# Retention from block 8 on by chunks of 64 tokens, with the state stacked under the values, in a fused retention and maxout kernel

## The chip, the cores and the metric

One core of a Trainium2 chip runs the whole kernel. The metric is the time of one execution on the device, in microseconds (us). The engines are called as in the profile: PE is TensorE (PEld its weight loads), DVE VectorE, ACT ScalarE, POOL GpSimd and SP SyncE, which issues nearly all DMAs.

## What is computed

Eight sequences of 576 tokens with 8 heads of 64 go through retention: causal attention without softmax, in which a key that lies r tokens back is weighted by gamma to the power r. Its output, 4608 tokens by 512, is the input of a feed-forward layer that takes the largest of three products.

```python
def _attn_ref(q, k, v):                      # 8 x 8 x 576 x 64 each
    scores = scale * np.matmul(q, k.transpose(0, 1, 3, 2))
    gamma = 1.0 - 2.0 ** (-5.0 - np.arange(H))
    rel = pos[:, None] - pos[None, :]
    Dmat = np.where(rel >= 0, gamma[:, None, None] ** rel[None, :, :], 0.0)
    return np.matmul(scores * Dmat, v)

def _moe_ref(x, w1, w2, w3, w_out):          # x: 4608 x 512, w: 512 x 768, w_out: 768 x 512
    h = np.maximum(np.maximum(x @ w1, x @ w2), x @ w3)
    return h @ w_out
```

All data is fp32. The weights come as 64-bit floats and are converted in the kernel.

## The kernel before

**Blocks and tiles.** The 4608 tokens are 36 blocks g of C = 128; four blocks make one tile t of NT = 512 tokens, nine in all. Blocks do not line up with the sequences: a sequence is four and a half blocks. While the feed-forward work of tile t runs (`ffn`, L618), the retention of tile t + 1 is woven into it. `steps(t)` (L731) writes that order out by hand: twelve slots per tile, and the loop at the end (L771) runs the calls of a slot and then lets `ffn` go on to its next `yield`. From tile 1 on, 120 of PE's fp32 products, spread over six feature blocks `fb` of 20 each (`up`, L559), stand between slots 0 and 9; slots 10 and 11 lie in `downs` (L407). Nothing is reordered afterwards: each engine executes its instructions in the order in which this Python code issues them.

**Retention of one block before.** The decay is split into a factor of the key's position (`gk`), one of the query's position (`gq`), and a causal mask. `load` brings k, v (and, up to block 6, q) with tokens on the partitions; `load_blocks` (L187) brings q and k a second time in 32 by 32 blocks, so that DVE's block transpose gives `qT` and `kT` with the head's dimension on the partitions (`transposes`, L220; up to block 6 PE transposes instead). `decay_values` (L212) multiplies v by `gk` on POOL to give `vd`. `scores` (L236) makes eight products kT qT, 64 rows by 128 columns of weights with 128 columns moving, in two PSUM banks, and DVE multiplies each bank by the causal mask into `st`. `state` (L255) makes K^T vd, eight products with 64 columns moving, and `keep` (L266) adds it to the running state on DVE and multiplies the sum by gamma^128 (`gs`) on POOL. `values` (L284) makes the output of two blocks: `vd` times `st` (L299, eight products for each block), the next states' products (L263), and the state times `qT` (L312, eight for each block, over the queries whose sequence began in an earlier block); `output` multiplies the two banks by `gq` on DVE into `xT`, and after the last block of a tile adds the 13 sums of X that the fast matrix product of the feed-forward layer needs (L343).

**Who works when.** `soon` (L180) puts DVE steps of retention, and the loads, in a queue `urgent`; `chore` takes one out between products (L663 sets how often), and `scores` and `values` empty the queue first. `up` leaves its partial products in the banks of `ps_x` and `ps_y` (two each); ACT copies them to `part` tiles (20 in turn), and DVE joins these (L568). Retention has the four banks of `ps_r`.

Of the kernel before, what the change touches and what calls it, by code (L numbers as in the profile page):

```python
# [48 lines left out]
C = 128  # L49
NT = 4 * C  # L50
NH = NT // 2
BY_PE = 7
AHEAD = 3
FILL = 224
# [26 lines left out]
def kernel(  # L81
# [24 lines left out]
    assert B * S % C == 0 and S >= C and N % NT == 0 and NT % P == 0 and 2 * D == P and NP == NDC  # L106
# [3 lines left out]
    vpool = ctx.enter_context(tc.tile_pool(name="vpool", bufs=3))  # L110
    att = ctx.enter_context(tc.tile_pool(name="att", bufs=2))
    stp = ctx.enter_context(tc.tile_pool(name="stp", bufs=4))
# [15 lines left out]
    gk = const.tile([C, H], FP32, name="gk")  # L128
    one, top, inf, first = (const.tile([P, 1], FP32, name=n) for n in ("one", "top", "inf", "first"))
    const.tile([P, FILL // 4], FP32, name="fill")  # L130
    gq = const.tile([P, 2, NP // 2, C], FP32, name="gq")
    gs = const.tile([P, NP, D], FP32, name="gs")
# [18 lines left out]
    def start_of(g):  # L151
        r = -g * C % S
        return r if r < C else None

    masks = {0: causal, None: causal}
    for r in sorted({start_of(g) for g in range(NG)} - {0, None}):
        m = masks[r] = const.tile([C, C], FP32, name=f"causal{r}")
        nc.gpsimd.tensor_copy(m[:], causal[:])
        nc.gpsimd.memset(m[0:r, r:C], 0.0)


    raws, vds, qks, sts, states, kvs = {}, {}, {}, {}, {}, {}
# [10 lines left out]
    late, chores, urgent, spread = {}, deque(), deque(), []  # L173
# [13 lines left out]
    def load_blocks(g, *blocks):  # L187
        for n, src in (("q", q), ("kx", k)):

            if 0 in blocks:  # L190
                raws[n, g] = raw.tile([P, NP, C // 32, 32], FP32, tag=n, name=n + "raw", bufs=2)
            t = raws[n, g]
            for blk in blocks:
                b, pos = divmod(g * C + 32 * blk, S)
                for a in range(4):
                    nc.sync.dma_start(
                        t[32 * a:32 * a + 32, :, blk, :],
                        src[b, a // 2::2, pos:pos + 32, 32 * (a % 2):32 * (a % 2) + 32].rearrange("p j i -> j p i"))

    def load(g):  # L200
        if g >= BY_PE and ("q", g) not in raws:
            load_blocks(g, *range(C // 32))
        for n, src in (("k", k), ("q", q), ("v", v)) if g < BY_PE else (("k", k), ("v", v)):
            if n == "v" and g == CPT - 1:
                load_weights(1)
            bufs = 3 if n == "k" else 2
            pool, bufs = (raw0, 1) if g < BY_PE and g % (bufs + 1) == bufs else (raw, bufs)
            t = raws[n, g] = pool.tile([C, H, D], FP32, tag=n, name=n + "raw", bufs=bufs)
            for row, b, pos, m in spans(g):
                nc.sync.dma_start(t[row:row + m], src[b, :, pos:pos + m, :].rearrange("h p d -> p h d"))  # L210

    def decay_values(g):  # L212
        t = vds[g] = vpool.tile([C, H, D], FP32, tag="vd", name="vd")
        nc.gpsimd.tensor_tensor(t[:], raws.pop(("v", g))[:], gk[:].unsqueeze(2).to_broadcast([C, H, D]),  # L214
                                op=ALU.mult)
# [4 lines left out]
    def transposes(g):  # L220
        both = qks[g] = {}
        if g >= BY_PE:
            for n in ("k", "q"):
                t = both[n] = att.tile([P, NP, C], FP32, tag=n + "T", name=n + "T", bufs=2 if n == "k" else 3)
                soon(partial(nc.vector.transpose, t[:].rearrange("a p c -> a (p c)"),
                             raws.pop(("kx" if n == "k" else n, g))[:].rearrange("a p b i -> a (p b i)")))
            return
        for n, src in (("k", raws["k", g]), ("q", raws.pop(("q", g)))):
            pool, tag = (ps_r, "r") if g >= CPT else (ps_x, "x")
            pt = pool.tile([P, NP, C], FP32, tag=tag, name=n + "t")  # L230
            for p in range(NP):
                nc.tensor.transpose(pt[:, p, :], pair(src, p), ident[:C, :C])
            t = both[n] = att.tile([P, NP, C], FP32, tag=n + "T", name=n + "T", bufs=2 if n == "k" else 3)
            nc.scalar.copy(t[:], pt[:])

    def scores(g):  # L236
        chore(len(urgent))
        qT, kT = qks[g]["q"], qks[g]["k"]
        s = [ps_r.tile([C, NP, C], FP32, tag="r", name=f"s{j}") for j in range(2)]
        for p in range(NP):  # L240
            for j in range(2):
                r = slice(D * j, D * (j + 1))
                nc.tensor.matmul(s[j][:, p, :], lhsT=kT[r, p, :], rhs=qT[r, p, :], start=True, stop=True)  # L243
        st = sts[g] = att.tile([C, 2, NP, C], FP32, tag="st", name="st", bufs=2)
        for j in range(2):
            soon(partial(nc.vector.tensor_tensor, st[:, j], s[j][:],
                         masks[start_of(g)][:].unsqueeze(1).to_broadcast([C, NP, C]), op=ALU.mult))
# [4 lines left out]
    def half(j):  # L252
        return slice(D * j, D * (j + 1))
# [12 lines left out]
    def keep(g):  # L266
        def step(t, kv):
            if start_of(g) is not None:
                nc.vector.tensor_tensor(t[:], kv[:], gs[:], op=ALU.mult)
            else:  # L270
                nc.vector.tensor_tensor(t[:], kv[:], states[g][:], op=ALU.add)  # L271
                nc.gpsimd.tensor_tensor(t[:], t[:], gs[:], op=ALU.mult)  # L272

        if begins(g):
            t = states[g + 1] = stp.tile([P, NP, D], FP32, tag="state", name="state")
            soon(partial(step, t, kvs[g]))
# [7 lines left out]
    def values(chunks, new_states=(), later=False):  # L284
# [7 lines left out]
        t, i = divmod(chunks[0], CPT)  # L292
        pool, tag = (ps_r, "r") if chunks[0] >= CPT - 1 else (ps_y, "y")
        o = [pool.tile([P, len(chunks), NP // 2, C], FP32, tag=tag, name="o") for _ in range(2)]
        for m, g in enumerate(chunks):
            for n in range(NP):
                for c in range(2):
                    h = head(c, n)
                    nc.tensor.matmul(o[n % 2][half(c), m, n // 2, :], lhsT=vds[g][:, h, :],  # L299
                                     rhs=sts[g][:, h % 2, h // 2, :], start=m == 0 and n < 2,  # L300
                                     stop=before(g) == 0, skip_group_check=True)
# [20 lines left out]

    def output(chunks, o, t, i):
# [8 lines left out]
        i += len(chunks) - 1  # L332
# [285 lines left out]
    def ffn(t):  # L618
# [36 lines left out]
        for n, fb in enumerate(order):  # L655
            if fb not in plain:
                while fb // 2 not in summed_fp:
                    chore()
            steps_of_one = up_plain_all(t, h, fb) if fb in plain else up(t, h, fb)
            for step, cost in enumerate(steps_of_one):  # L660
                if fb in plain:
                    chore(4 if (fb, step) == (plain[-1], 1) else 8)
                elif step % 2 or step % 5 == 4:  # L663
                    chore(len(urgent) > 0)
                elif step % 4 == 2 and chores:
                    chores.popleft()()
                count += cost or 1
                if count * (NF // 2 * 3) >= (parts + 1) * total:
                    parts += 1
                    yield  # L670
            if n % 2:
                sums_of_hidden(h, fb // 2)
                if fb in plain:
                    weight_sums(fb // 2)
        chore(len(urgent))
        for n, _ in enumerate(downs(t, h)):
            chore(4)
            if n in (1, 3):
                yield
# [17 lines left out]
    decay_values(0)  # L697
# [7 lines left out]
    decay_values(1)  # L705
# [6 lines left out]
    decay_values(2)  # L712
# [4 lines left out]
    decay_values(3)  # L717
# [10 lines left out]
    decay_values(CPT)  # L728
    convert(2)

    def steps(t):  # L731
# [4 lines left out]
        def at(n, *what):  # L736
            for step, *args in what:
                if step is values:
                    if args[0][0] < NG:
                        todo[n].append(partial(values, args[0], [g for g in args[1] if g < NG]))  # L740
# [3 lines left out]
        if t == 1:  # L744
# [3 lines left out]
            at(2, (transposes, b), (decay_values, b), (load, c))  # L748
            at(3, (scores, b), (load_blocks, d, 0))
            at(4, (decay_values, c), (load_blocks, d, 1, 2))  # L750
            at(5, (values, [a, b], [b, c]), (load_blocks, d, 3), (load, d))
            at(6, (keep, c), (transposes, c), (load_blocks, d + 1, 0))
            at(7, (transposes, d), (decay_values, d), (load_blocks, d + 1, 1, 2))
            at(8, (scores, c), (scores, d), (load_blocks, d + 1, 3), (load, d + 1))
            at(9, (load_blocks, d + 2, 0, 1))
            at(10, (decay_values, d + 1), (load_blocks, d + 2, 2))
            at(11, (values, [c, d], [d, d + 1]), (load_blocks, d + 2, 3), (load, d + 2),
               (transposes, d + 1))
            return todo
        for n in range(0, CPT, 2):  # L760
            a, b, m = CPT * t + n, CPT * t + n + 1, 6 * (n // 2)
            at(m, (keep, a), (transposes, b), (decay_values, b))
            if a == 2 * CPT:
                at(m, (load, a + 2))
            at(m, (load, b + 2))
            at(m + 2, (scores, a), (scores, b))
            at(m + 3, (decay_values, a + 2))
            at(m + 4, (values, [a, b], [b, a + 2]), (transposes, a + 2), (load, a + 4))
# [59 lines left out]
```

## Time and profile before

| | |
|---|---|
| median of three runs | 775.72 us (775.42 to 776.01) |
| span of the profiled execution | 773.3 us |
| PE, weight loads, DVE, ACT, POOL busy | 766.8, 626.5, 564.1, 325.9, 102.9 us |
| granted TensorE clock | 1.000 throughout |
| DMA | 59.33 MB, queues busy 35% of 16 engines' span |
| one tile of feed-forward, from tile to tile | 81.9 to 82.6 us |

The profile is of one execution; the span runs from its first to its last instruction. PE and PEld are one engine seen twice: the weight load of a product overlaps the product before it. Each fp32 product of the program is two records on PE and two on PEld, so a line with x32 is 16 products. The end of a PE record is modelled, so the distance between starts says more than its length. In a timeline, a line's length runs from the first start to the last end of a merged group, and neighbouring lines overlap a little.

### The profile page before, as it was taken

How to read it: one execution, taken by the hardware profiler on the slowest of the kernel's cores; microseconds unless marked ns; L12 is line 12 of the kernel's file. 1: busy time of each engine (PE TensorE's matmuls, PEld its weight loads, DVE VectorE, ACT ScalarE, POOL GpSimd, SP SyncE). 2: the span in 40 equal slices, each digit the busy share in tenths (PEclk: the TensorE clock that was granted, in tenths of full speed). 3: DMA queues.
4: the chain of work that ended last, by engine and by line, in shares of the span. 5: the costliest groups of instructions: out<-in, count | busy, mean ns of one | idle time of the engine just before them, and what ended most of it. 6: DMA issues, size and time to landing. Idle time of an engine off the chain costs nothing.

```text
span 773.3 us, 14511 instructions
## 1 busy us (share of the span) xinstructions
PE 766.8 (99%) x5032; PEld 626.5 (81%) x5032; DVE 564.1 (73%) x1249; ACT 325.9 (42%) x811; POOL 102.9 (13%) x124
## 2 busy tenths in 40 slices
PE   9999999999999999999999999999999999999998
PEld 8545454688888888888888888888888888888887
DVE  3898989799577856784768757876778568845672
ACT  3665631163254415451346234532544054514551
POOL 2210021111110201111111111110112001200000
PEclk9999999999999999999999999999999999999999
DMA  9995544333333332333233333333333323001001
GB/s 225 241 226 131 158 110 103 59 58 58 92 58 58 57 77 62 56 75 67 62 56 58 59 96 58 57 58 96 58 56 59 84 48 74 3 15 42 2 1 55
DMA packets 237083, 59.33 MB, mean 77 GB/s; under 512 B 217937, under 2 KB 235729, under 8 KB 237009
## 3 DMA queue, kind: packets, MB, share of 16 engines
q1 hardware_dynamic: 236432, 58.07, 34.9%
q8 instruction: 39, 0.64, 0.3%
q10 hardware_dynamic: 576, 0.33, 0.1%
q14 instruction: 36, 0.29, 0.1%
HBM read 48.89 MB, written 9.44 MB: 75 GB/s over the span
## 4 chain that ended last, share of the span: by engine, by line
PE 97%; SPq 1%; DVE 1%; DMA 1%; issue 0%; ACT 0%; DVEq 0%
PE a L588 18%; PE b L588 16%; PE dx L428 11%; PE up L611 11%; PE c L588 8%; PE dz L428 5%; PE d L588 5%; PE e L588 5%; PE s L243 4%; PE o L299 4%; PE down L598 3%; PE dy L428 3%; PE o L312 2%; PE kv L263 2%; SPq L210 1%; DMA qraw<-in_q_dram 1%
## 5 line engine op out<-in xcount | busy, mean ns | idle before, releaser
L568 DVE TENSOR_TENSOR part<-part 128x256 f32<-128x256 f32 x460 | 208.7, 462 | 78.2 <-ACT part L573 70.4
L573 ACT COPY part<-b 128x256 f32<-128x256 f32 x230 | 85.6, 372 | 126.0 <-PE b L588 114.6
L573 ACT COPY part<-a 128x256 f32<-128x256 f32 x276 | 102.7, 372 | 84.9 <-PE a L588 72.3
L214 POOL TENSOR_TENSOR vd<-vraw,gk 128x512 f32<-128x512 f32 x36 | 40.3, 1120 | 339.2 <-DMA vraw<-in_v_dram 219.9
L611 PE MATMUL up<-xT,w 128*128 128x512 f32 (+2 forms) x200 | 84.7, 578 | 0.3 <-DVE w L517 0.3
L588 PE MATMUL a<-s,w 128*128 128x256 f32 x276 | 82.3, 380 | 0.0
L588 PE MATMUL b<-s,n 128*128 128x256 f32 x276 | 82.1, 379 | 0.0
L611 PEld LDWEIGHTS up<-xT,w 128*128 128x128 f32 x200 | 36.8, 190 | 42.3 <-issue 39.2
L588 PEld LDWEIGHTS b<-s,n 128*128 128x128 f32 x276 | 52.4, 190 | 7.1
L588 PEld LDWEIGHTS a<-s,w 128*128 128x128 f32 x276 | 52.3, 190 | 7.3 <-issue 0.2
L588 PE MATMUL c<-xT,w 128*128 128x256 f32 x184 | 56.0, 386 | 0.0
L588 PE MATMUL b<-xT,n 128*128 128x256 f32 x184 | 55.4, 382 | 0.0
L588 PE MATMUL d<-s,w 128*128 128x256 f32 x184 | 55.1, 381 | 0.0
L568 DVE TENSOR_TENSOR h<-part 128x256 f32<-128x256 f32 x92 | 42.6, 463 | 6.6
L588 PE MATMUL e<-xT,w 128*128 128x256 f32 x184 | 47.3, 379 | 0.0
L588 PE MATMUL a<-xT,n 128*128 128x256 f32 x184 | 47.2, 379 | 0.0
L428 PE MATMUL dx<-To,H 128*128 128x256 f32 (+1 forms) x204 | 44.9, 370 | 0.0
L435 ACT COPY part<-dx 128x256 f32<-128x256 f32 (+1 forms) x34 | 10.5, 363 | 80.1 <-PE dx L428 77.9
L178 DVE TENSOR_TENSOR xT<-o,gq 128x512 f32<-128x512 f32 x28 | 18.1, 686 | 33.3 <-PE o L312 33.3
L428 PEld LDWEIGHTS dx<-To,H 128*128 128x128 f32 x204 | 36.6, 190 | 5.5 <-issue 1.0
L243 PEld LDWEIGHTS s<-qT,kT 64*128 64x128 f32 x576 | 33.9, 188 | 7.9 <-PE b L588 4.0
L272 POOL TENSOR_TENSOR state<-state,gs 128x256 f32<-128x256 f32 x24 | 18.6, 776 | 162.1 <-DVE state L271 162.1
(104 smaller groups left out, 1299.8 us busy)
## 6 DMA issues: line engine op xcount, KB each, us to landing
bits<-in_moe_w_dram SPq DMA_DIRECT2D x36, 256.0 KB, 5.6
out_dram<-osb SPq DMA_DIRECT2D x35, 256.0 KB, 2.1
kraw<-in_k_dram SPq DMA_DIRECT2D x32, 256.0 KB, 3.0
vraw<-in_v_dram SPq DMA_DIRECT2D x32, 256.0 KB, 3.4
qraw<-in_q_dram SPq DMA_DIRECT2D x464, 16.0 KB, 1.8
kxraw<-in_k_dram SPq DMA_DIRECT2D x464, 16.0 KB, 1.8
bits<-in_moe_w_out_dram SPq DMA_DIRECT2D x6, 512.0 KB, 4.7
qraw<-in_q_dram SPq DMA_DIRECT2D x6, 256.0 KB, 4.1
```

Of the source, the lines that this page charges most:

```text
L178: (urgent or chores).popleft()()
L214: nc.gpsimd.tensor_tensor(t[:], raws.pop(("v", g))[:], gk[:].unsqueeze(2).to_broadcast([C, H, D]), op=ALU.mult)
L243: nc.tensor.matmul(s[j][:, p, :], lhsT=kT[r, p, :], rhs=qT[r, p, :], start=True, stop=True)
L263: nc.tensor.matmul(kvs[g][half(h % 2), h // 2, :], lhsT=kr[r:, h, :], rhs=vds[g][r:, h, :], start=True, stop=True)
L272: nc.gpsimd.tensor_tensor(t[:], t[:], gs[:], op=ALU.mult)
L299: nc.tensor.matmul(o[n % 2][half(c), m, n // 2, :], lhsT=vds[g][:, h, :], rhs=sts[g][:, h % 2, h // 2, :], start=m == 0 and n < 2, stop=be ...
L428: nc.tensor.matmul(o, lhsT=hS[n](fp)[:, m * P:(m + 1) * P], rhs=late["T"][n][:, fp, cols], start=first and fp == 0 and (m == 0 or last and ...
L568: nc.vector.tensor_tensor(out, a, b, op=op)
L573: nc.scalar.copy(t[:], ps[step[0]][:])
L588: nc.tensor.matmul(ps[chain][:], lhsT=factor(w, fb), rhs=xS[t][x], start=n == 1, stop=ends, skip_group_check=True)
L598: nc.tensor.matmul(b[:], lhsT=h[:, fb, m * P:(m + 1) * P], rhs=w_sb["out", fb], start=(fb == 0), stop=(fb == NF - 1))
L611: nc.tensor.matmul(ps[:, cols], lhsT=w_sb[i, fb][:, dc * P:(dc + 1) * P], rhs=xT[t][:, dc, cols], start=dc == 0 and cols.start == 0, stop= ...
```

## The change

Blocks 0 to 7 keep the code described above. From block 8 on (`BY_CHUNKS = 8`) each block is two chunks of 64 tokens, c = 0 and 1, and a chunk never crosses a sequence's start, since 576 is nine chunks.

For each chunk a tile `va{c}` of 128 rows holds the chunk's values in its half c and the state before the chunk in the other half. A second tile `m{c}` holds the masked scores in half c and the transposed queries in the other half. One product of the two over all 128 rows then gives scores times values and state times queries together. The transposed q and k are loaded so that chunk 0 lies in rows 64 to 127 and chunk 1 in rows 0 to 63, all eight heads side by side.

`chunk_scores` makes four products per head, each 64 by 64 with 64 columns moving, one in each quadrant of PE's array: K^T V of chunk 0 and of chunk 1, and the scores of chunk 1 and of chunk 0. They write two banks, `sk0` and `sk1`, each of which holds K^T V of one chunk in one half and the scores of the other chunk in the other half. K, not V, now carries the key's decay: `decay` multiplies k in place, by one instruction on POOL for blocks 8 and 9 and by eight instructions on ACT for each later block, taken from a new queue `scaling`. The mask `gm` carries the same factor for the scores. `keep_chunk` adds K^T V to the old state on DVE, into the other half of the next chunk's `va` tile (a copy on ACT for the first chunk of a sequence, nothing for its last); gamma^128 is multiplied in by POOL after the odd chunk.

The slots change too: scores stand one slot earlier (not for blocks 8 and 9), values at the slot three after them, and in tiles from 2 on `chore` is called less often unless more than six steps wait.

```diff
 NT = 4 * C
 BY_PE = 7
+BY_CHUNKS = 8
-FILL = 224
+FILL = 192
...
-    vpool = ctx.enter_context(tc.tile_pool(name="vpool", bufs=3))
-    att = ctx.enter_context(tc.tile_pool(name="att", bufs=2))
-    stp = ctx.enter_context(tc.tile_pool(name="stp", bufs=4))
+    vpool = ctx.enter_context(tc.tile_pool(name="vpool", bufs=4))
+    att = ctx.enter_context(tc.tile_pool(name="att", bufs=3))
...
-    gs = const.tile([P, NP, D], FP32, name="gs")
+    gs = ppool.tile([P, NP, D], FP32, tag="part", name="gs")
+    gm = const.tile([P, H, D], FP32, name="gm")
...
+                c, e = divmod(blk, 2)
+                for a in range(2):
+                    r = D * (1 - c) + 32 * a
                     nc.sync.dma_start(
+                        t[r:r + 32, :, e, :],
+                        src[b, :, pos:pos + 32, 32 * a:32 * a + 32].rearrange("h p i -> p h i"))
+
+    def stacked(g, c):
+        if (g, c) not in vas:
+            vas[g, c] = vpool.tile([P, H, D], FP32, tag=f"va{c}", name=f"va{c}")
+        return vas[g, c]
...
+            if n == "v" and g >= BY_CHUNKS:
+                for c in range(2):
+                    b, pos = divmod(g * C + D * c, S)
+                    nc.sync.dma_start(stacked(g, c)[half(c)], v[b, :, pos:pos + D, :].rearrange("h p d -> p h d"))
+                continue
...
+    def decay(g):
...
+        kr = raws["k", g]
+        if spread:
+            scaling.extend(partial(nc.scalar.mul, kr[:, h, :], kr[:, h, :], gk[:, h:h + 1]) for h in range(H))
+        else:
+            nc.gpsimd.tensor_tensor(kr[:], kr[:], factor, op=ALU.mult)
+        for c in range(2):
+            if place(g, c) == 0:
+                nc.gpsimd.memset(vas[g, c][half(1 - c)], 0.0)
...
     def scores(g):
         chore(len(urgent))
+        scale(len(scaling))
+        if g >= BY_CHUNKS:
+            chunk_scores(g)
+            return
...
+    def chunk_scores(g):
+        kT, kr = qks[g]["k"], raws.pop(("k", g))
+        sk = [ps_r.tile([P, H, D], FP32, tag="r", name=f"sk{j}") for j in range(2)]
+        nc.scalar.copy(ms[g, 0][half(1)], ms[g, 1][half(1)])
+        for h in range(H):
+            for c in range(2):
+                if place(g, c) < S // D - 1:
+                    nc.tensor.matmul(sk[c][half(c), h, :], lhsT=kr[half(c), h, :], rhs=vas[g, c][half(c), h, :],
+                                     start=True, stop=True)
+            for c in (1, 0):
+                r = half(1 - c)
+                nc.tensor.matmul(sk[1 - c][half(c), h, :], lhsT=kT[r, h, :], rhs=ms[g, 1][r, h, :],
+                                 start=True, stop=True)
+        def mask(c):
+            nc.vector.tensor_tensor(ms[g, c][half(c)], sk[1 - c][half(c)], gm[half(c)], op=ALU.mult)
+        def keep_chunk(c):
+            to = stacked(g + c, 1 - c)
+            if place(g, c) == 0:
+                nc.scalar.copy(to[half(c)], sk[c][half(c)])
+            else:
+                nc.vector.tensor_tensor(to[half(c)], sk[c][half(c)], vas[g, c][half(1 - c)], op=ALU.add)
+            if c:
+                nc.gpsimd.tensor_tensor(to[half(1)], to[half(1)],
+                                        gs_of[half(1)].unsqueeze(2).to_broadcast([D, H, D]), op=ALU.mult)
+        for c in range(2):
+            soon(partial(mask, c))
+        for c in range(2):
+            if place(g, c) < S // D - 1:
+                soon(partial(keep_chunk, c))
...
+    def key_masks():
+        for c in range(2):
+            nc.gpsimd.tensor_tensor(gm[half(c)], causal[half(c), half(c)].unsqueeze(1).to_broadcast([D, H, D]),
+                                    gk[half(c)].unsqueeze(2).to_broadcast([D, H, D]), op=ALU.mult)
...
+    def chunk_values(chunks, t, i):
+        outs = [ps_r.tile([P, 2, NP // 2, C], FP32, tag="r", name="o") for _ in chunks]
+        for g, o in zip(chunks, outs):
+            for m in range(2):
+                for n in range(NP):
+                    for c in range(2):
+                        h = head(c, n)
+                        nc.tensor.matmul(o[half(c), n % 2, n // 2, half(m)], lhsT=vas[g, m][:, h, :],
+                                         rhs=ms[g, m][:, h, :], start=m == 0 and n == 0, stop=True,
+                                         skip_group_check=True)
...
+            soon(partial(nc.vector.tensor_tensor, x, o[:], gq[:], op=ALU.mult))
...
-                elif step % 2 or step % 5 == 4:
+                elif step % 2 and (step % 4 == 1 or t == 1 or len(urgent) > 6) or t == 1 and step % 5 == 4:
                     chore(len(urgent) > 0)
...
+                if step % 3 == 2:
+                    scale()
...
-            at(m, (keep, a), (transposes, b), (decay_values, b))
-            if a == 2 * CPT:
-                at(m, (load, a + 2))
-            at(m, (load, b + 2))
-            at(m + 2, (scores, a), (scores, b))
-            at(m + 3, (decay_values, a + 2))
-            at(m + 4, (values, [a, b], [b, a + 2]), (transposes, a + 2), (load, a + 4))
+            first_pair = a == BY_CHUNKS
+            s = m + 2 if first_pair else m + 1
+            at(m, (transposes, b))
+            if first_pair:
+                at(m, (decay, b), (load, a + 2), (carry, a))
+            at(s, (scores, a), (scores, b), (load, b + 2))
+            at(s + 1, (decay, a + 2))
+            at(s + 2, (decay, b + 2))
+            at(s + 3, (values, [a, b]), (transposes, a + 2), (load, a + 4))
```

At the start of the program POOL also makes the mask `gm` (`key_masks`, between the decays of blocks 0 and 1), ACT copies the 64-row factors `gs_of` out of `gs`, and the values of blocks 0 to 7 are loaded into `va0` tiles and decayed into `va1` tiles.

## The prediction

> **What bounds the kernel now.** I read the page first: busy time, the clock row and the chain that ended last.
>
> ```profile
> PE 766.8 (99%) x5032; PEld 626.5 (81%) x5032; DVE 564.1 (73%) x1249; ACT 325.9 (42%) x811; POOL 102.9 (13%) x124
> PEclk9999999999999999999999999999999999999999
> PE 97%; SPq 1%; DVE 1%; DMA 1%; issue 0%; ACT 0%; DVEq 0%
> ```
>
> PE is busy all the time at a full clock, and 97% of the chain is PE executing, not waiting. So the time is the sum of PE's stream, and a change is worth what it takes out of that stream, as long as the other engines keep up. "Busy" alone does not show this, since ends are modelled; the timeline of PE does. Here are a pair's scores and a pair's values:
>
> ```profile
> 219.21 0.59 PE L588 MATMUL a<-s,w 128*128 128x256 f32 x2
> 219.74 2.06 PE L243 MATMUL s<-qT,kT 64*128 64x128 f32 x32
> 221.72 0.70 PE L588 MATMUL c<-xT,w 128*128 128x256 f32 x2
> ```
>
> ```profile
> 233.05 0.59 PE L588 MATMUL d<-s,w 128*128 128x256 f32 x2
> 233.57 1.97 PE L299 MATMUL o<-st,vd 128*64 128x128 f32 x32
> 235.47 1.30 PE L263 MATMUL kv<-vd,kraw 64*64 64x64 f32 x32
> 236.70 0.90 PE L312 MATMUL o<-qT,state 64*64 64x128 f32 x32
> 237.53 0.70 PE L588 MATMUL b<-xT,n 128*128 128x256 f32 x2
> ```
>
> In an unbroken stream a 256-column record starts 0.216 us after the last. The price of a section is thus the distance from the last product record's end before it to the first one's end after it, less 0.216. For the scores: the last record before starts at 219.43 and runs 0.38, the first after starts at 221.72 and runs 0.48 (it loads its weights uncovered), which gives 222.20 - 219.80 - 0.216 = **2.18 us**. All 14 pairs of scores from block 8 on cost this. The 14 sections of values, measured in the same way, cost 3.13 to 4.15 us (fewer products where a sequence begins or ends), together 53.6 us. So blocks 8 to 35 take 14 x 2.18 + 53.6 = **84.2 us** of PE, 6.0 a pair. That is all that this change can touch.
>
> **PE: what goes and what comes.** The starts of the single records give the pace of each form. Scores: two rows of the array at once, a couple of records every 0.111 us; 16 couples are 1.78, so 0.40 of the 2.18 us is for changing the array's division on the way in and out. L299: couples every 0.110. L263 (64 columns moving): couples every 0.058. L312 uses all four quadrants: with 128 columns four records start 6 to 7 ns apart, then the next four 0.110 us after the first four; with 64 columns (the second block of the pair, from 237.18 on) the fours follow each other every **0.058 us**.
>
> New scores of a pair: 2 blocks x 8 heads x 4 = 64 products = 128 records, every one 64 by 64 with 64 columns moving, and consecutive ones always in different quadrants. This is the form of the last 16 records of L312. 32 fours x 0.0585 = 1.87 us, plus 0.40 for entry and exit as now. Scores of the second block wait for a PE semaphore again before they start; I add 0.10 for that. 2.37 us, against 2.18.
>
> New values of a pair: 2 x 16 products = 64 records of 128 rows, 64 columns, 64 moving, the form of L263's second block (128*64 128x64), so 32 couples x 0.058 = 1.87, plus 0.40: 2.27 us, against 3.83 on average.
>
> Sum of a pair 4.64 us; 14 pairs 65.0; the saving is 84.2 - 65.0 = **19.2 us**. Between ends: entry and exit at 0.25 to 0.30 each and no wait between blocks gives 4.3 a pair, a saving of 24; 0.6 each gives 5.0 a pair, a saving of 14. I take 0.40, which is what the row of the scores shows.
>
> **A rule against it.** The Trainium skill's page "TensorE: Matmul & The Clock Gate" ("Wait — 56ns, not 53.3ns?") says that matmuls never start less than about 25 ns apart, however few columns move. By that rule the 128 records of a pair's scores take 3.2 us, not 1.87; a pair then costs 3.2 + 0.5 + 2.27 = 5.97, and nothing is gained. The trace disagrees: four records start within 20 ns, and 16 of them take 0.19 us from first start to last, 12 ns each. I take the row, but it shows only four fours in succession, just after slower records during which PE's queue could fill. That 32 fours keep this pace is the boldest step here, and the first rival below.
>
> **DVE.** Per block before: two masks (0.68 us each), two transposes (0.70, 0.67), one state sum (0.41 for 256 columns), one `xT` (0.69). After: two masks of 64 rows by 512, two transposes, one `xT`, and two `keep_chunk` of 64 by 512. A 64-row instruction over 512 columns has no row; between half (if rows counted) and the 0.68 of 128x512, I take 0.68, because the rows differ by columns (256: 0.41, 512: 0.68) and nothing shows that rows count. So +0.95 us a block, less the sequence's first and last chunk, about +3.4 us a tile:
>
> ```profile
> 350.41:432.49 82.08, 82.08 (x566) 71.67 (x565) 59.51 (x134) 33.85 (x92) 11.73 (x14) 1.00 0.32 65
> 412.00:428.00 16.00, 16.00 (x97) 13.94 (x96) 15.16 (x33) 8.19 (x23) 2.78 (x3) 1.00 0.27 44
> ```
>
> The columns after the window's length are PE, PEld, DVE, ACT and POOL. DVE goes from 59.5 of 82.1 to about 62.9 of 79.3, 79%: enough on average, but the second row shows 16 us in which it is already 95% busy while PE still streams. The skill's "TensorEngine Tiling (Array Packing)" ("PSUM Bottleneck") warns that tiling speeds up TensorE but not the emptying of PSUM. Here that means eight 64-row instructions after each pair's scores where four masks stood. Worked out: eight at 0.60 from start to start (as in the rows of masks that follow one another) are 4.8 us, one feature block's 14 joins at 0.34 to 0.42 are 4.8 to 5.9; together 9.6 to 10.7, while PE does 2.4 + 20 x 0.432 = 11.0 us. What is late first is the join that frees the bank of product e for product d, due 19 products after the scores (about 10.5 us); in the order of issue 15 DVE instructions stand before it (six of retention, nine joins), so it ends about 8 to 9 us after the scores begin. It holds by 1 to 2 us. I cost it at nothing; without that cover each pair loses up to 1 us.
>
> **ACT.** 26 blocks x 8 multiplications of 128x64. No row; between COPY 128x1 (0.19) and 128x256 (0.37) in proportion, an estimate of 0.24. With one 64x512 copy a block (0.59 by the 128x512 copy) this is 2.5 us a block, 10 a tile: 34 to 44 of 79. They are issued one per three products, so a bank's copy is put off by at most 0.24. The joins' slack hides it; all 16 are issued before the scores that need them. Nothing on the path.
>
> **POOL.** `vd` (1.13) and three of four state factors (0.76) go; one 64x512 factor a block comes, 1.13 by the nearest row. It stands between the first block's second `keep_chunk` and the second block's first; in DVE's order about twelve instructions (5 us) lie between. Hidden. At the start `key_masks` (two, about 2.2 us) goes into POOL's idle time between 6.9 us and 9.4 us, where it waits for the next v; a few tenths late at most, and PE is then waiting for DMAs anyway. `gs_of` adds two tiny ACT copies. 0 to +0.5 us, taken as 0.
>
> **DMA, SP, slots.** Bytes and pieces of q and k are the same, in half as many issues; v comes in two issues instead of one. Loads stay about a pair ahead, and no PE row waits on a DMA after the start. Values stay in slots 4 and 10; scores one slot earlier give DVE 13 more products. The thinner `chore` delays only steps that `scores` and `values` flush. Nothing.
>
> **Sum.** 773.3 - 19.2 = 754.1 us of span. The median of the runs lies 2.4 above the profiled span, so **756.5 us**.
>
> **Rivals.** (1) *Four quadrants don't keep four-wide pace* over 128 records, and scores go in couples at 0.058. Then scores cost 3.74 + 0.5, a pair 6.5 against 6.0, +7 us: **783**, slower. Everything else being so, it decides from about 0.10 us a four. For it: no stretch here asks PE for so many short instructions in a row; against it: L312's own fours. 8%. (2) *PE's issue limits at about 25 ns a record*: 774 to 775, no change. 5%. (3) *DVE (or ACT behind it) becomes the limit* after each pair's scores: 0.6 to 1 us of PE idle a pair, 8 to 14 us: **765 to 770**. For it: the 95% stretch; against it: the margin counted above. 14%. (4) *The likeliest*, 750 to 762: 73%.
>
> The range takes in (4) and (3), 750 to 770. A measurement here can tell 0.2%, about 1.6 us, from no change. Faster is (3) and (4) and a little of (2): 0.88; same 0.03; slower 0.09.
>
> **What would show it.** Right: scores and values sections of about 2.4 and 2.3 us in PE's timeline, fours every 0.058; tiles 79 to 79.5 us apart; PE still 99%. Wrong: records of the new scores starting in couples (rival 1) or evenly at 25 ns (2); PEld waiting for DVE or ACT at products d, a or b some ten products after the scores (3); POOL's factor ahead of a waiting `keep_chunk`; or any row of PE waiting for `kraw`, which ACT now decays.

## The result and the profile after

The changed kernel takes 769.76 us (four runs, 769.25 to 770.31) against 775.57 us before on the same chip: a ratio of 0.9924, 95% interval 0.991 to 0.9938. It is faster by 5.8 us. The forecast was 756.5 us, a gain of 19.2 us, in a range of 750 to 770: the sign was right, the gain three times too large, and the result lies at the far end of the range, where the prediction had put its rival 3.

The page after, with the rows that answer to those shown of before:

```profile
span 767.8 us, 16109 instructions
PE 752.8 (98%) x5928; PEld 607.8 (79%) x5928; DVE 588.8 (77%) x1268; ACT 388.8 (51%) x1057; POOL 91.7 (12%) x112
PEclk9999999998999999999999999999999999999999
PE 86%; DVE 9%; SPq 1%; issue 1%; DMA 1%; ACT 1%; DVEq 0%
```

PE was 97% of the chain that ended last and is 86% now; DVE has come in with 9%. One slice of the clock row shows an 8. So PE's own work has shrunk, but PE waits.

First, PE's new sections. These are the values of one pair in PE's timeline, and, from the view by line, the scores of the pair before them (the window held one pair; first and last start are given):

```profile
237.89 0.59 PE L713 MATMUL d<-s,w 128*128 128x256 f32 x2
238.41 2.09 PE L436 MATMUL o<-m,va 128*64 128x64 f32 x64
240.43 0.48 PE L713 MATMUL b<-xT,n 128*128 128x256 f32 x1
```

```profile
L321 PE MATMUL sk<-m,kT x64: 217/219/268, 217.6 to 219.5; 64*64 64x64 f32 x64
L317 PE MATMUL sk<-va,kraw x48: 217/219/268, 217.6 to 219.4; 64*64 64x64 f32 x48
```

Priced as in the prediction, all 14 sections of values cost 2.21 us, and the sections of scores 2.21 to 2.32 with one of 2.76. Together they take 63.0 us where the old ones took 84.2. **PE's work fell by 21.2 us**, a little more than forecast.

Then, what was lost. I add up, over all neighbouring product records outside retention, the distance of their starts beyond 0.216 us for each 256 columns, and call this PE's excess. Before it is 3.2 us in the whole execution; after it is 18.9. The balance closes: -21.2 + 15.7 = -5.5, and the span went from 773.3 to 767.8. Of the 15.7 us, 6.6 lie in tile 1 and 9.1 in tiles 2 to 7. The waits of PE and PEld say for whom (columns: us in total, times, longest):

```profile
PE d L713 <- DVE part L693: 5.3, 9, 3.6
PE a L713 <- ACT part L698: 2.8, 4, 1.4
PEld d L713 <- DVE part L693: 10.9, 14, 4.0
PEld a L713 <- ACT part L698: 6.4, 14, 1.8
```

The products c, d and e take the two banks of `ps_y` in turn. Product d waits for the bank of e, which a join on DVE has to read first; product a waits for a bank that ACT has to copy. Neither row existed before at this size.

**How DVE came to be late.** This is DVE's timeline from one pair's scores (PE 217.6 to 219.7) to the join of e, with gaps and their releasers in brackets:

```profile
218.86 1.41 DVE L325 TENSOR_TENSOR m<-sk,gm 64x512 f32<-64x512 f32 x2 [0.78 <-PE sk L321]
220.30 1.41 DVE L333 TENSOR_TENSOR va<-sk,va 64x512 f32<-64x512 f32 x2
221.74 2.07 DVE L693 TENSOR_TENSOR part<-part 128x256 f32<-128x256 f32 x3
223.91 0.43 DVE L693 TENSOR_TENSOR h<-part 128x256 f32<-128x256 f32 x1
224.26 0.88 DVE L693 TENSOR_TENSOR part<-part 128x256 f32<-128x256 f32 x2
225.16 0.68 DVE L325 TENSOR_TENSOR m<-sk,gm 64x512 f32<-64x512 f32 x1
225.77 0.87 DVE L693 TENSOR_TENSOR part<-part 128x256 f32<-128x256 f32 x2
226.74 1.17 DVE L693 TENSOR_TENSOR h<-part 128x256 f32<-128x256 f32 x1
227.95 0.69 DVE L325 TENSOR_TENSOR m<-sk,gm 64x512 f32<-64x512 f32 x1
228.67 0.42 DVE L693 TENSOR_TENSOR part<-e,part 128x256 f32<-128x256 f32 x1
```

and POOL in the same stretch:

```profile
221.84 1.23 POOL L335 TENSOR_TENSOR va<-va,gs_of 64x512 f32<-64x512 f32 x1 [26.16 <-PE b L713]
226.59 1.04 POOL L335 TENSOR_TENSOR va<-va,gs_of 64x512 f32<-64x512 f32 x1 [3.52 <-ACT va L331]
```

DVE has hardly a gap from 218.9 to 229.1. The join of e ends 11.5 us after the scores' first record here; its median over tiles 2 to 7 is 10.8 us. PE wants the bank after about 10.2: 2.05 us to the first product after the scores, and 19 products of 0.43. Where POOL multiplies a state, one DVE join next to it takes 0.7 us longer (2.07 us for three where 1.34 is usual, 1.17 for an h). POOL's second factor is early in this pair because a sequence begins in it (its sum is ACT's copy); in the pair at 378 us, where none begins, only one factor falls before the join of e, which ends after 10.8 us. PE shows the result at product d, which starts at 229.15, 0.35 us late. In nine of the twelve pairs of tiles 2 to 7 this d is 0.27 to 0.43 us late, and in four the d one feature block later by up to 0.18.

**Product a.** In the pair at 498 us the copy that starts a sequence's state (L331, on ACT) stands between two copies of PE's banks. ACT's timeline, then PE's:

```profile
505.38 0.37 ACT L698 COPY part<-b 128x256 f32<-128x256 f32 x1
507.14 0.58 ACT L331 COPY va<-sk 64x512 f32<-64x512 f32 x1 [1.39 <-DVE m L325]
507.62 0.36 ACT L698 COPY part<-a 128x256 f32<-128x256 f32 x1
```

```profile
506.04 0.59 PE L713 MATMUL b<-s,n 128*128 128x256 f32 x2
508.04 0.70 PE L713 MATMUL a<-s,w 128*128 128x256 f32 x2 [1.41 <-ACT part L698]
```

ACT takes its instructions in order. L331 waits 1.39 us for a mask of DVE on the same bank, the copy of a waits behind it, and PE behind that. Four such stalls cost 0.5 to 1.6 us each.

**Tile 1.** The largest stall of all, and what followed it, in PE's timeline and in the view by stretches (after the length: PE, PEld, DVE, ACT, POOL busy, clock, DMA share, GB/s):

```profile
181.08 0.66 PE L713 MATMUL a<-s,n 128*128 128x256 f32 x2
185.37 1.22 PE L713 MATMUL d<-s,w 128*128 128x256 f32 x2 [3.63 <-DVE part L693]
...
185.40:190.60 5.20, 5.20 (x12) 4.18 (x13) 3.56 (x10) 1.92 (x6) 0.33 (x1) 0.50 0.31 70
```

In tile 1 DVE also makes the weight sums for later tiles, and four of these ran between 170.1 and 182.7 us, while the pair's scores began at 170.3 and its join of e at 184.9. PE waited 3.6 us, and then ran at half its clock for 5.2 us, which cost another 2.7.

### The profile page after: what moved, and what is told of

Same layout as the page of the kernel before. It is cut to its first block, busy times and chain, and to the rows that moved or that the text cites. A ratio compares the mean times of both kernels' runs of the same rounds, so it can differ in the third digit from the quotient of the medians.

```text
span 767.8 us, 16109 instructions
## 1 busy us (share of the span) xinstructions
PE 752.8 (98%) x5928; PEld 607.8 (79%) x5928; DVE 588.8 (77%) x1268; ACT 388.8 (51%) x1057; POOL 91.7 (12%) x112
## 4 chain that ended last, share of the span: by engine, by line
PE 86%; DVE 9%; SPq 1%; issue 1%; DMA 1%; ACT 1%; DVEq 0%
PE a L713 15%; PE b L713 13%; PE dx L553 11%; PE up L736 11%; PE c L713 6%; PE dz L553 5%; PE d L713 5%; PE e L713 4%; DVE part L693 4%; PE o L436 4%; PE down L723 3%; PE dy L553 3%; DVE m L325 2%; PE sk L317 2%; PE sk L321 1%; DVE h L693 1%
## 5 line engine op out<-in xcount | busy, mean ns | idle before, releaser
L186 ACT ACTIVATE kraw<-kraw,gk 128x64 f32<-128x64 f32 x208 | 66.9, 349 | 0.3
L713 PE MATMUL d<-s,w 128*128 128x256 f32 x184 | 57.2, 393 | 5.4 <-DVE part L693 5.3
L335 POOL TENSOR_TENSOR va<-va,gs_of 64x512 f32<-64x512 f32 x24 | 26.3, 1098 | 262.1 <-DVE va L333 164.5
L713 PE MATMUL b<-xT,n 128*128 128x256 f32 x184 | 57.6, 395 | 0.0
L713 PEld LDWEIGHTS d<-s,w 128*128 128x128 f32 x184 | 34.3, 193 | 15.0 <-DVE part L693 10.9
L693 DVE TENSOR_TENSOR h<-part 128x256 f32<-128x256 f32 x92 | 40.6, 441 | 6.9
L325 DVE TENSOR_TENSOR m<-sk,gm 64x512 f32<-64x512 f32 x56 | 38.5, 688 | 8.4 <-PE sk L321 7.2
L560 ACT COPY part<-dx 128x256 f32<-128x256 f32 (+1 forms) x34 | 10.5, 362 | 63.4 <-PE dx L553 61.2
L698 ACT COPY part<-d 128x256 f32<-128x256 f32 x92 | 34.2, 372 | 14.3 <-PE d L713 10.3
```

The costliest lines, as they stand in the source:

```text
L186: scaling.popleft()()
L325: nc.vector.tensor_tensor(ms[g, c][half(c)], sk[1 - c][half(c)], gm[half(c)], op=ALU.mult)
L335: nc.gpsimd.tensor_tensor(to[half(1)], to[half(1)], gs_of[half(1)].unsqueeze(2).to_broadcast([D, H, D]), op=ALU.mult)
L560: nc.scalar.copy(both[m][:, cols], o)
L693: nc.vector.tensor_tensor(out, a, b, op=op)
L698: nc.scalar.copy(t[:], ps[step[0]][:])
```

## The experiments

Unless said otherwise each edit is to the changed kernel. Each run was timed beside the kernel before on its own chip, and the chips differ between rows, so the ratios compare more safely than the times. "Join of e" is its end after the first record of a pair's scores, median over tiles 2 to 7; the other two columns are from the profiled execution.

| run | time, us | ratio to before (95%) | PE's excess | retention | join of e |
|---|---|---|---|---|---|
| before | 775.6 | | 3.2 | 84.2 | |
| the change | 769.8 | 0.9924 (0.991 to 0.9938) | 18.9 | 63.0 | 10.8 |
| scores apart | 763.7 | 0.9853 (0.9838 to 0.9868) | 9.2 | 67.0 | 8.8 |
| no state factor | 761.7 | 0.9821 (0.9805 to 0.9837) | 11.1 | 62.4 | 10.0 |
| first copy on DVE | 766.1 | 0.988 (0.9864 to 0.9897) | 14.1 | 63.7 | |
| tile 1's weight sums | 768.1 | 0.9907 (0.9892 to 0.9922) | 14.9 | 63.3 | |
| queue not emptied | 769.4 | 0.992 (0.9902 to 0.9938) | 16.8 | 63.0 | 10.0 |
| the three together | 766.7 | 0.9882 (0.9867 to 0.9896) | 14.5 | 63.2 | |
| no key decay on ACT | 769.3 | 0.9915 (0.9897 to 0.9934) | 18.3 | 62.8 | |
| old chore rate | 770.5 | 0.9939 (0.9921 to 0.9956) | 18.8 | 63.0 | |
| second block later | 761.1 | 0.981 (0.9795 to 0.9824) | 9.2 | 63.0 | 9.3 |
| later, and two edits | 758.8 | 0.9784 (0.9768 to 0.9801) | 7.1 | 62.9 | 9.3 |
| factor on ACT | 798.4 | 1.029 (1.0275 to 1.0306) | 46.3 | 62.3 | |
| mended, no factor | 755.3 | 0.9723 (0.9702 to 0.9744) | 4.6 | 62.3 | |

**Scores apart.**

```diff
-            at(s, (scores, a), (scores, b), (load, b + 2))
-            at(s + 1, (decay, a + 2))
+            at(s, (scores, a), (load, b + 2))
+            at(s + 1, (scores, b), (decay, a + 2))
```

> The changed kernel, with the second block's scores of a pair one slot (13 products) after the first block's, instead of right behind them. Theory (DVE falls behind because eight 64-row instructions and POOL's two factors come in one burst ahead of the joins that free PE's banks): PE's excess time between products, 15.7 us more than before in the changed kernel, falls by a third to two thirds; 760 to 765 us. Rival A (ACT is the limit, by its 208 multiplications of 0.35 us in the queue of bank copies): unchanged, 769 to 771. Rival B (only the one long stall in tile 1 and the state-start copies on ACT matter): 763 to 769, with the 0.3 to 0.4 us waits of product d in the later tiles still there.

763.7 us, as the theory said. The waits of product d are gone from tiles 2 to 7, and of the stalls at a one of 0.3 us is left. It pays for that: 14 more entries into the divided array raise retention from 63.0 to 67.0 us, 0.29 each.

**No state factor.**

```diff
-            if c:
-                nc.gpsimd.tensor_tensor(to[half(1)], to[half(1)],
-                                        gs_of[half(1)].unsqueeze(2).to_broadcast([D, H, D]), op=ALU.mult)
```

> The changed kernel without POOL's multiplication of the state by gamma^128 (left out, so the state is not decayed). Theory (POOL's 1.1 us instruction holds up DVE joins with two SBUF inputs for about 0.75 us, twice a pair, in the middle of the burst): DVE reaches the join of e 1 to 1.5 us sooner after each pair's scores, the waits of product d shrink or vanish, 764 to 767 us. Rival A (ACT's load): 769 to 771. Rival C (DVE's own eight instructions are too many, POOL adds nothing): 769 to 770, the long join rows stay.

761.7 us, better than the theory's 764, though the join of e comes only 0.8 us sooner, not 1 to 1.5. DVE joins of over 0.55 us, after the first 130 us, fall from 39 to 12. The waits of d vanish in tiles 2 to 7; the stalls at a stay, two of them at half their size. Besides its hold on DVE this also takes away the wait of the second block's state sum for POOL, so not every microsecond of the 8 is shown to be the hold.

**First copy on DVE.**

```diff
-                nc.scalar.copy(to[half(c)], sk[c][half(c)])
+                nc.vector.tensor_copy(to[half(c)], sk[c][half(c)])
```

> The changed kernel with the copy that starts a sequence's state (7 in all) on DVE instead of ACT. Theory (this copy stands in ACT's queue and waits for a late mask of DVE on the same bank, so that ACT cannot empty the banks of a and b behind it): the waits of product a right after b (0.70, 0.52, 1.57 and 0.68 us in the profile) go, 766 to 767 us. Rival (DVE's length of queue alone decides, wherever the copy stands): no gain, 769.5 to 771.

766.1 us. All four stalls at a after b are gone, the waits of d are as before. The two are separate.

**Tile 1's weight sums.**

```diff
-                elif step % 4 == 2 and chores:
+                elif step % 4 == 2 and chores and not (t == 1 and urgent):
```

> The changed kernel; in tile 1 a weight sum is taken out of its queue only while no retention step waits, so these sums move behind the burst or into tile 2. Theory (the 3.8 us stall of product d in tile 1, and the half clock for 5 us after it, come from the burst plus five weight sums on DVE at the same time): the stall falls below 1 us and the clock stays full, 763 to 765 us. Rival (the stall comes from the burst alone): stall still over 2 us, 768 to 771. Rival (the sums are only late somewhere else): a new stall in tile 2 before feature block 2, 767 to 771.

A part of it: the stall shrinks from 3.8 to 2.65 us and the clock stays full. In the trace tile 1 loses 3.7 us of excess, but the time only 1.7. The first products of tile 0 began 3.0 us later in this profile; over all runs they begin between 24.5 and 27.7 us, whatever the edit, so a microsecond or two of a single profile is the start's. The forecast of 763 to 765 was missed: most of the stall is the burst itself.

**Queue not emptied**, and the same with the two edits above it.

```diff
     def scores(g):
-        chore(len(urgent))
+        if g < BY_CHUNKS or g % 2 == 0:
+            chore(len(urgent))
...
-            at(s, (scores, a), (scores, b), (load, b + 2))
+            at(s, (scores, a), (load, b + 2), (scores, b))
```

> The changed kernel; the second block's scores stay right behind the first's, but the queue of DVE steps is not emptied between them, so that the eight steps of a pair go to DVE one by one between the joins (the load of block b + 2 is queued before the second scores). Theory (the order on DVE is the cause: eight steps, 0.7 us each, and two POOL factors come ahead of the join that frees the bank of e): product d no longer waits in tiles 2 to 7, PE's retention sections stay at 63 us where the run with scores apart paid 67 for its extra changes of the array's division, and the time is 759 to 763 us. Rival (total load of DVE, in whatever order): 765 to 770 us, the waits move to other products. Rival (ACT): 769 to 771.

> The same order as in the run before it, plus the state-start copy on DVE and the weight sums of tile 1 behind waiting retention steps. Theory: the three waits are separate and their gains add; 757 to 760 us, which would be nearly the whole of PE's saving of 21 us. Rival (one queue, one backlog: once the order is mended the other two edits bring nothing): equal to the run before within 1 us.

769.4 and 766.7 us: both theories missed, and the first number is what the rival of total load said; the run of the second block below decides against that rival. DVE's timeline shows why an even spread did not help:

```profile
378.61 0.68 DVE L326 TENSOR_TENSOR m<-sk,gm 64x512 f32<-64x512 f32 x1 [0.78 <-PE sk L322]
381.38 1.34 DVE L694 TENSOR_TENSOR part<-part 128x256 f32<-128x256 f32 x3 [2.09 <-ACT part L699]
...
386.24 1.41 DVE L334 TENSOR_TENSOR va<-sk,va 64x512 f32<-64x512 f32 x2
387.68 0.42 DVE L694 TENSOR_TENSOR part<-e,part 128x256 f32<-128x256 f32 x1
```

Right after the scores DVE's next joins wait for products that PE has yet to do. In the changed kernel the first block's steps fill this hole; here they stand behind the joins, DVE idles 2.1 us, and the steps come later in front of the join of e.

**No key decay on ACT** (`decay` without the `scaling` multiplications) and **old chore rate** (`elif step % 2 or step % 5 == 4`).

> The changed kernel without ACT's 208 multiplications of k by the key's decay (left out, so the states are wrong from block 10 on). Rival A (ACT's load makes PE wait): 759 to 764 us. Theory (DVE's order): ACT's instructions hold a bank's copy by 0.25 us at a time and this is hidden; 768.5 to 770 us.

> The changed kernel with the old rule for taking steps out of the queue (twelve of twenty products instead of five, or ten while more than six wait). Theory: the second block's masks and sums come even closer to the join of e, so the waits of product d grow; 771 to 775 us. Rival (the thinner rule makes DVE late): 763 to 768 us. No effect: 769 to 770.

769.3 and 770.5 us, neither clear of the changed kernel (their intervals overlap). ACT's 208 multiplications cost nothing. With the old rule the waits of d did grow, as the theory said, to about 1.2 us in four pairs, but three of the four stalls at a went, and PE's excess is 18.8 against 18.9: the rule shifts the loss and is neither its cause nor a cure. That it would cost 1 to 5 us was wrong.

**Second block later.** The first block's steps go out at once, into the hole; the second block's wait for eight products.

```diff
+        if g % 2:
+            hold[0] = 8
         for c in range(2):
             soon(partial(mask, c))
...
+                elif hold[0]:
+                    hold[0] -= 1
                 elif step % 2 and (step % 4 == 1 or t == 1 or len(urgent) > 6) or t == 1 and step % 5 == 4:
                     chore(len(urgent) > 0)
...
-            at(s, (scores, a), (scores, b), (load, b + 2))
+            at(s, (scores, a), (load, b + 2), (scores, b))
```

> The changed kernel; the first block's four DVE steps still go out at once (DVE has nothing else then), but the second block's four wait for eight products, until the join of e has been issued (the load of block b + 2 goes ahead of the second scores). Theory (not DVE's total load but what stands ahead of the join of e, and that only where DVE has no idle time left): 1.4 us of masks move behind the join, the waits of product d (0.3 to 0.4 us, twice a tile) vanish in tiles 2 to 7, PE's sections stay at 63 us, 764 to 767 us with the stalls of tile 1 and of the state-start copies left. Rival (total load, as the run with the queue not emptied suggests): the waits only move by one feature block, 768 to 771 us.

> The order of the run before it, with the state-start copy on DVE and tile 1's weight sums behind waiting steps. Theory: the three causes add, 758 to 761 us, better than the scores apart (763.7). Rival: not more than 1 us better than the run before it, or a stall reappears in tile 1 or 2.

761.1 us, better than the 764 to 767 expected, and 758.8 with the state-start copy on DVE and the weight sums behind. DVE in the corresponding pair of the latter:

```profile
215.55 2.07 DVE L696 TENSOR_TENSOR part<-part 128x256 f32<-128x256 f32 x3
217.72 0.42 DVE L696 TENSOR_TENSOR h<-part 128x256 f32<-128x256 f32 x1
218.06 1.68 DVE L696 TENSOR_TENSOR part<-part 128x256 f32<-128x256 f32 x4
219.84 0.42 DVE L696 TENSOR_TENSOR h<-part 128x256 f32<-128x256 f32 x1
220.30 0.42 DVE L696 TENSOR_TENSOR part<-e,part 128x256 f32<-128x256 f32 x1
220.64 0.67 DVE L326 TENSOR_TENSOR m<-sk,gm 64x512 f32<-64x512 f32 x1
```

No mask stands between the joins any more, and the join of e ends at 220.72, 9.3 us after the scores in the median: in time. The two masks that moved behind it are 1.4 us, and so much earlier does it end (10.8 to 9.3). DVE's busy time in the whole execution is no smaller than in the changed kernel (596.1 us against 588.8), so it was what stood ahead of that join, not DVE's total. The rival was right in part: in tiles 4 to 7 a wait of 0.5 to 0.7 us at product d remains, one feature block later. 758.8 us is the best version found that computes everything.

**Factor on ACT** (to the run before): each state factor as eight ACT instructions of 64x64, two after a product, instead of one on POOL.

> The run before it, with gamma^128 multiplied in by eight ACT instructions of 64x64 instead of one on POOL. Theory (POOL's instruction holds up a DVE join by about 0.75 us, 28 times, while ACT's load costs nothing, as the run without its multiplications showed): 2 to 5 us less than the run before it. Rival (in ACT's queue the eight hold up the bank copies, or wait for DVE's sum at the head of the queue): 1 to 6 us more.

798.4 us, slower than before the change; the rival won, by far more than it said. The waits of PE and of ACT:

```profile
PE a L726 <- ACT part L711: 23.3, 20, 3.3
ACT va L193 <- DVE va L341: 36.1, 13, 7.3
```

ACT's load was free; ACT's order is not. A factor at the head of its queue waits up to 7.3 us for DVE's sum, and every bank copy behind it waits too.

**Mended, no factor.**

> The best order so far (second block's steps later, state-start copy on DVE, weight sums behind) without POOL's multiplication by gamma^128 (left out, so the state is not decayed). In the changed kernel leaving it out was worth 8 us. Theory (POOL's hold on DVE joins costs only where DVE has no time left, and the mended order gave it time): PE's excess falls from 7.1 us to 4 to 5.5, and the time by 1.5 to 3 us, to 756 to 757.5. Rival (POOL's hold costs the same in any order): 6 us or more, 751 to 753. Rival (nothing left of it): 758 to 759.

755.3 us: 3.5 us less (4.7 by the ratios), a little more than the 1.5 to 3 expected, where it was 8 in the changed kernel. What POOL holds up costs less once DVE's order leaves room, but it is not gone.

## Why the prediction was wrong

- **PE, right.** Scores 2.37 forecast, 2.21 to 2.32 measured but for one section; values 2.27 and 2.21; sum 65.0 and 63.0. The boldest step held: 32 fours in succession keep four-wide pace. In the section at 257.9 us 128 records start within 1.90 us, 15 ns each, so the rule of 25 ns between starts does not bound matmuls in different quadrants. (Half of the sections, like the one in the view above, have 112 records, 16 fours and 16 threes, because a sequence's last chunk needs no state; the prediction counted 128 in all. They take as long, since a three goes at the pace of a four.) Rivals 1 and 2 fell.
- **DVE's amount, right.** 62.9 us a tile forecast, and in the tile that answers to the one shown before:

```profile
351.92:431.55 79.63, 79.45 (x694) 68.74 (x692) 62.58 (x136) 43.31 (x129) 9.64 (x13) 1.00 0.35 71
```

- **The step that failed** is "It holds by 1 to 2 us. I cost it at nothing": the join of e, forecast at 8 to 9 us after the scores begin and due at 10.5, ends at 10.8 in the median and is due at about 10.2. Three terms of that sum were too small. In the timeline shown, the six 64-row steps take up to 0.72 us of DVE each, not 0.60 (four from 218.86 to 221.71). The nine joins take 0.46, not 0.34 to 0.42, when POOL's part is taken off. And POOL's factor, which I checked only as something that DVE waits for, adds 0.7 us: twice in the pair shown, once in the pair at 378 us. With the cover gone I had put the loss at "up to 1 us" a pair; measured in tiles 2 to 7 it is 9.1 us over 12 pairs, 0.76 each, at products d and a together. So rival 3, at 14% and 765 to 770 us, is what happened.
- **Seen from one side only: the place of the scores.** "scores one slot earlier give DVE 13 more products" counts the time up to the values; to product d the distance became shorter. Before, in tiles from 2 on, the d that takes the bank of e came 26 products after the scores (13.3 us from their first record) in one pair of a tile, and only after the `downs`, some 35 us on, in the other. Now it comes after 19 products in both. How much of the lost cover this is stays open, because no run moves the scores of both blocks back; "scores apart" moves the second block's, and the waits of d went.
- **Not foreseen at all:** the state-start copy on ACT (listed in the change, and costed only as 0.59 us of ACT time, not as a wait at the head of a queue), and tile 1, where I did not look at what else DVE had to do. They come to some 3.5 us and 6.6.
- **ACT, right as load.** The multiplications take 0.35 us (0.24 estimated), and removing them changes nothing.
- **Start and chore rule, right.** The first product of tile 0 begins at 24.67 us, against 24.61; the old rule brings no gain.

With the order mended the kernel comes to 758.8 us, 2.3 above the forecast: the saving was there, and the cover was not.

## What to carry to other kernels

When PE is the bound and its work shrinks, count for every engine that frees PE's banks what stands ahead of the freeing instruction in its order, over the very stretch that gets shorter; an average of 79% busy says nothing there. Put steps that nobody waits for soon behind that instruction, but use the hole in which the engine would wait anyway for the ones that are ready. And read each instruction added to an in-order engine twice: as time, and as a wait in front of everything behind it.

## What the runs showed of the hardware

- After the 3.63 us stall in tile 1 (3.8 us from start to start, beyond 0.216) PE ran at a granted clock of 0.50 for 5.2 us. The Trainium skill's page "TensorE: Matmul & The Clock Gate" (Part 1) has the clock halved after an idle window of about 3.4 us; here stalls of 2.9 us by starts (without the state factor, clock 0.54 over the next 3.3 us; with it on ACT, 0.53 over 3.4) were also followed by a stretch at half pace, one of 2.65 us was not (1.00). With what follows, the stalls of 3.8 and 2.9 us cost 1.4 to 1.7 times their length.
- A POOL multiplication of 1.1 us lengthens a neighbouring DVE join of two `part` tiles by about 0.7 us. Instructions that read an operand from a PSUM bank were not lengthened: in the changed kernel's trace 11 masks and 18 joins of e or c ran beside a multiplication or a sum of POOL for 0.2 us or more and took 0.68 to 0.70 and 0.41 to 0.43 us, as elsewhere.
- A 64-row DVE instruction over 512 columns takes 0.688 us, the same as 128 rows (0.684).
- Entry into and exit from the divided array cost about 0.3 us together (14 more sections: 4.0 us).
